# A two-layer transformer kernel: a wide second mixer buffer in dead key and value slots, VectorE score tiles across segment borders, and a new plan

## The chip, the cores and the metric

The kernel runs on one core of one Trainium2 chip. The metric is the time of one launch in device microseconds; the median of several runs counts. The core has five engines that run side by side: TensorE (PE; its weight loads are PEld in the profile), VectorE (DVE), ScalarE (ACT), GpSimd (POOL) and SyncE (SP), which here only issues DMAs.

## The reference

The input x has 2048 rows of 448 values in bfloat16. Two equal layers are run one after the other, each an attention block (16 heads of 28 values) and a mixer block with an MLP:

```python
x = A_x
x = x + _A_ref(_layernorm(x), A_wqkv, A_wo)
x = x + _B_ref(_layernorm(x), B_w1, B_w2, B_w3, B_w4)
x = x + _A_ref(_layernorm(x), A_wqkv, A_wo)
x = x + _B_ref(_layernorm(x), B_w1, B_w2, B_w3, B_w4)

def _A_ref(x, wqkv, wo):            # q, k, v: 16 heads of 28
    scores = einsum("bhqd,bhkd->bhqk", q, k) * (28 ** -0.5)
    o = einsum("bhqk,bhkd->bhqd", softmax(scores), v)
    return o.reshape(B, S, D) @ wo

def _B_ref(x, w1, w2, w3, w4):
    h = gelu(layernorm(x) @ w1)     # then four column groups of h, moved by
    hs = shifted(h) @ w2            # +1, -1, +2, -2 rows, with zeros at the ends
    x1 = x + hs
    return x1 + gelu(layernorm(x1) @ w3) @ w4      # w3: 448 x 1792, w4: 1792 x 448
```

## The kernel before

The 2048 rows are 16 tiles of 128 rows. Heads go in 4 groups of 4. The queries are cut into five chunks (of 4, 4, 4, 2 and 2 tiles), and keys are taken in passes, so that attention can begin before all keys exist; one chunk, one head group and one pass make a **segment**. There are 28 segments in layer one (0 to 27) and 36 in layer two (28 to 63). A segment has one block for each 512 columns of scores and head: a key tile for a chunk of 4 query tiles, two key tiles for a chunk of 2.

*The stream of scores.* `t_scores` walks the segments in order and takes units of 3 and 2 score tiles of 128x512 in turn (banks 0 to 2, 3 and 4 of PSUM). `score_ops` issues their matmuls (L1300). `t_exp` (L1455) lets ScalarE take the exponential of each unit, PSUM to the buffer PT. `t_pv` multiplies with the values (L761; its buffer named PT or PD) into bank 5. `t_norm` copies the sums out (L1534, L1536) and, after the last pass of a chunk, divides, mostly through two DMAs and a product on GpSimd (L1560), in the last chunk of layer two through TensorE.

*Tiles for VectorE.* Beside a unit, `t_scores` may take one or two more score tiles for VectorE: it looks 5 to 6 blocks ahead (DLO, DHI) **in the same segment**, only for chunks of 4 tiles, and only if TensorE's planned fillers of the last 8 us make up a share of at least FTH. It takes one if fewer tiles of the segment were taken than the rate D_RATE times (block + 1) times 4, and if a free bank (b6, b7), an integer buffer (`yd`, 2) and an output buffer (`PD`, 4) are at hand. `d_first` (L1341) brings the scores out of PSUM as fixed-point numbers, and `d_chain` (L1362, L1364, L1366, L1369) works the exponential out as a polynomial on the low half and an exponent from the high half: five VectorE instructions. The chain has the priority DPRIO until its block is near, then 1.0.

*The mixers.* When a chunk is done in all four head groups, `t_outproj` multiplies with wo and adds to x; `t_mixA` (LayerNorm, w1, gelu through a tanh, L1684 to L1704) works on the chunk, `t_mixB` on groups of 3, 4, 4, 2 and 3 tiles, whose rows need their neighbours: the shifted product with w2 (x1b, L1772), LayerNorm (L967), transposing, w3 into `h2T` (evacuated by VectorE, L1837), one long gelu on ScalarE over the whole buffer (L1852; it needs another activation table, loaded before and after), and w4. There is one `h2T` of 14 x 512 columns. In layer two the group of 2 tiles uses instead a buffer `h2V` of 14 x 256 columns in value slots 9 to 15, which are dead from the end of layer one's attention ("kvfree"). The last group runs after the exponentials, with its hidden values in PT. Each `t_mixA`, `t_mixB`, key and query load holds one of the transposed buffers xT0, xT1 and, after "kvfree", xT2 in key slots 9 to 12.

*Keys and values of layer two.* `kT` and `vaug` have 23 slots of one tile. Layer one uses 0 to 15; layer two puts its tiles 0 to 6 into 16 to 22 and 7 to 15 into 0 to 8. So slots 16 to 22 are empty in most of layer one, and 9 to 15 in layer two. `t_kv` loads transposed tiles by a DMA on SP's queue; `k_proj` makes keys (evacuation L1110, squares on GpSimd L1096, their sum on TensorE, the maximum on VectorE L1121), `v_proj` the values.

*The plan.* All of this is written as Python generators, and a planner (`Sched`) orders their instructions in one list for each engine before the launch. It has a duration for each instruction, margins for what other engines deliver late (DOUBT, DOUBT2), a rank for each part (RANK: 'a' and 'b' the mixer halves, 'k' and 'q' the projections, by layer and index; lower goes first), a lead for the queries (Q_LEAD) and a share of TensorE's recent 2.3 us that must be work (TARGET). Where TensorE would be idle below that share, `keep_pe_busy` puts in a **filler** (L1893): four small matmuls into a bank that nobody uses.

## Time and profile before

| | |
|---|---|
| median of 8 runs | 1077.35 us (1076.23 to 1081.22) |
| the profiled execution | 1077.18 us |
| its span | 1075.5 us |
| granted TensorE clock, mean | 0.998 |
| exponentials L1455 | 805 instructions, 920.8 us on ScalarE |
| long gelus L1852 on h2T | 8 instructions, 41.9 us |
| table loads beside them | 8 before a gelu and 8 before an exponential, 1283 ns each |
| fillers L1893 | 3804 matmuls, 166.7 us |
| tiles on VectorE, L1341 | 37 |
| waits of ScalarE's exponentials for scores | 13.2 us in 10 waits, the longest 4.0 |

A row of the profile's groups gives the line, the engine and the operation, the tile written and those read, the shape and the count; then the busy time, the mean duration of one, and the idle time of the engine just before such instructions. Durations of neighbours overlap a little, so a busy time is less than count times mean. A row of stretches gives the busy time of each engine between two times, counted from the start of the span.

### The profile page before, as it was taken

To read this page: it belongs to the slowest core of one execution; us is meant where nothing else is said; L and a number is where in the kernel's file an instruction comes from. 1 tells how busy PE (TensorE), PEld (TensorE's weight loads), DVE (VectorE), ACT (ScalarE), POOL (GpSimd) and SP (SyncE) were. 2 spreads that over 40 slices of the span, in tenths; PEclk is the share of its full clock that TensorE was granted. 3 is DMA by queue.
4 is the path that set the end of the run, shared out by engine and by line. 5 is a ranking of instruction groups with operands and counts; after the bars stand their busy time and mean duration, and the time that the engine had idled before them with its cause. 6 is when DMAs were issued, how large, how long until landed. Compare 5 with 4: busy or idle time off the path is not lost.

```text
span 1075.5 us, 35352 instructions
## 1 busy us (share of the span) xinstructions
PE 1007.6 (94%) x16034; PEld 422.4 (39%) x16037; DVE 619.0 (58%) x1236; ACT 1020.7 (95%) x920; POOL 314.0 (29%) x506
## 2 busy tenths in 40 slices
PE   6899999999999999999999998999999999999998
PEld 2333443443333433343433433353333433444455
DVE  7776579836468336755156553514797484444442
ACT  6898999999999999999999999999999999999952
POOL 2244126201254024452042201102753130432111
PEclk9999999999999999999999999999999999999999
DMA  3547221103111022120221122413411110220000
GB/s 115 138 111 209 81 57 32 23 17 91 32 32 32 13 83 52 44 42 22 63 58 40 45 90 86 132 56 103 90 27 21 42 40 16 59 49 16 12 11 32
DMA packets 95494, 62.26 MB, mean 58 GB/s; under 512 B 68528, under 2 KB 85248, under 8 KB 95344
## 3 DMA queue, kind: packets, MB, share of 16 engines
q1 hardware_dynamic: 91968, 51.92, 18.8%
q0 software_dynamic: 3376, 8.09, 2.7%
q8 instruction: 125, 2.05, 0.8%
q14 instruction: 25, 0.20, 0.1%
HBM read 27.12 MB, written 15.71 MB: 40 GB/s over the span
## 4 chain that ended last, share of the span: by engine, by line
ACT 65%; PE 21%; DVE 11%; DMA 2%; issue 1%; POOL 0%; SPq 0%; DVEq 0%
ACT PT L1455 58%; PE ps L770 11%; PE ps L1300 5%; PE ps L761 4%; ACT h2T L1852 4%; DVE fb L1364 1%; DMA rT<-ub 1%; ACT fb L1703 1%; DVE PD L1369 1%; DVE fb L1362 1%; PE ps L1893 1%; ACT L1455 1%; ACT L1852 1%; DVE yd L1341 1%; DVE qT L1143 1%
## 5 line engine op out<-in xcount | busy, mean ns | idle before, releaser
L1455 ACT ACTIVATE PT<-ps 128x1536 bf16<-128x1536 f32 (+1 forms) x805 | 920.8, 1335 | 14.4 <-PE ps L1300 13.2
L1300 PE MATMUL ps<-qT,kT 32*128 32x512 bf16 (+1 forms) x2560 | 315.0, 340 | 29.4 <-ACT PT L1455 20.2
L761 PE MATMUL ps<-PT,vaug 128*32 128x512 bf16 (+1 forms) x2523 | 250.3, 340 | 0.0
L1300 PEld LDWEIGHTS ps<-qT,kT 32*128 32x128 bf16 x2560 | 80.7, 91 | 300.1 <-ACT PT L1455 272.9
L1893 PE MATMUL ps<-ident 128*32 128x256 bf16 x3804 | 166.7, 274 | 3.0 <-POOL ident L850 1.5
L770 PE MATMUL ps<-xT,w 128*32 128x512 bf16 (+2 forms) x1600 | 126.3, 360 | 2.8 <-DVE h2T L1837 1.4
L1893 PEld LDWEIGHTS ps<-ident 128*32 128x32 bf16 x3804 | 108.2, 96 | 30.3 <-issue 12.3
L770 PE MATMUL ps<-w,h2T 128*32 128x448 bf16 x1512 | 104.5, 359 | 13.8 <-ACT h2T L1852 12.9
L1837 DVE CAST h2T<-ps 128x512 bf16<-128x512 f32 (+2 forms) x112 | 67.9, 606 | 79.5 <-PE ps L770 69.9
L761 PEld LDWEIGHTS ps<-PT,vaug 128*32 128x32 bf16 x2523 | 74.7, 95 | 93.5 <-issue 80.2
L1560 POOL TENSOR_TENSOR otn<-ub,fb 128x512 bf16<-128x512 f32 (+1 forms) x36 | 40.6, 1128 | 183.4 <-DMA fb<-rscr 183.2
L1096 POOL TENSOR_TENSOR sq<-kT 128x512 bf16<-128x512 bf16 (+2 forms) x32 | 29.9, 937 | 120.4 <-DVE kT L1110 120.2
L770 PEld LDWEIGHTS ps<-xT,w 128*32 128x32 bf16 (+1 forms) x1600 | 43.7, 95 | 42.9 <-issue 17.9
L770 PEld LDWEIGHTS ps<-w,h2T 128*32 128x32 bf16 x1512 | 40.6, 97 | 50.8 <-issue 17.0
L1701 POOL TENSOR_TENSOR fb<-hT 112x512 f32<-112x512 bf16 (+1 forms) x36 | 37.4, 1042 | 78.2 <-DVE hT L1684 74.5
L1341 DVE TENSOR_SCALAR yd<-ps 128x512 int32<-128x512 f32 x37 | 25.1, 683 | 39.3 <-PE ps L1300 38.9
L1787 POOL TENSOR_TENSOR x_res<-x_res,x1b 128x448 f32<-128x448 f32 x32 | 38.9, 1224 | 20.9 <-DVE xn L967 19.3
L1534 DVE COPY ub<-ps 128x512 f32<-128x512 f32 (+1 forms) x40 | 23.3, 583 | 36.1 <-PE ps L761 35.8
L953 POOL TENSOR_SCALAR vpe<-mv 128x1 f32<-128x1 f32 (+2 forms) x21 | 5.5, 262 | 128.1 <-DVE mv L948 128.1
L1852 ACT ACTIVATE h2T<-h2T 128x7168 bf16<-128x7168 bf16 (+2 forms) x8 | 41.9, 5244 | 0.1
L1536 DVE SCALAR_TENSOR_TENSOR ub<-ub,fct,ps 128x512 f32<-128x512 f32 x24 | 17.9, 747 | 41.0 <-PE ps L761 40.7
L770 PE MATMUL ps<-kT,w 128*32 128x512 bf16 (+2 forms) x576 | 40.4, 360 | 0.8 <-DMA kT<-xn 0.7
(168 smaller groups left out, 1206.5 us busy)
## 6 DMA issues: line engine op xcount, KB each, us to landing
uscr<-ub SPq DMA_DIRECT2D x24, 256.0 KB
ub<-uscr SPq DMA_DIRECT2D x24, 256.0 KB
fb<-rscr SPq DMA_DIRECT2D x24, 256.0 KB
xnd<-xn SPq DMA_DIRECT2D x28, 128.0 KB, 2.2
x_res<-in_A_x_dram POOLq DMA_DIRECT2D x16, 224.0 KB, 4.2
xd<-x_res SPq DMA_DIRECT2D x16, 224.0 KB, 2.7
x_res<-xd SPq DMA_DIRECT2D x16, 224.0 KB, 3.6
out_dram<-obf SPq DMA_DIRECT2D x16, 112.0 KB
```

The lines of the kernel that those rows point to most:

```text
L761: return lambda e: e.matmul(out=out, lhsT=lhsT, rhs=rhs, start=start, stop=stop, **kw)
L770: r.append(e.matmul(out=out[c:c + w, :], lhsT=lhsT[:, c:c + w], rhs=rhs, start=start, stop=stop, tile_position=(0, c)))
L1096: return op("pool", 0.15 + NW * 0.0018, lambda e: e.tensor_tensor(out=sq[:, si, 0:NW], in0=src, in1=src, op=ALU.mult), reads=rk, writes=[( ...
L1300: yield op("pe", max(0.055, 0.22 / nc_ * NW / 512.0), lambda e, i=i, kc=kc, j=j, g=g, a=a, NW=NW, bank=bank: e.matmul(out=ps[:, bank, i * ...
L1341: yield op("dve", c_ps(512), lambda e: e.tensor_scalar(out=y, in0=ps[:, bi(bank), :], scalar1=SCALE * L2E * FS, scalar2=-126.0 * FS, op0=A ...
L1455: yield op("act", 0.06 + n * w * 0.000833, lambda e, bk=bk, s0=s0, n=n, w=w: e.activation(out=PT[:, s0:s0 + n, 0:w], in_=ps[:, bk[0]:bk[0] ...
L1560: yield op("pool", 0.2 + NW * 0.0021, lambda e: e.tensor_tensor(out=otn[:, g, 0:NW], in0=u, in1=rb[:, 0:NW], op=ALU.mult), reads=[uk, fk], ...
L1701: yield op("pool", 0.2 + NW * 0.00165, lambda e: e.tensor_tensor(out=f, in0=z, in1=z, op=ALU.mult), reads=hk, writes=[fk])
L1787: yield op("pool", 1.2, lambda e: e.tensor_tensor(out=X, in0=X, in1=X1, op=ALU.add), reads=[xk, ("x1b", s)], writes=[xk], deps=[nop_])
L1837: ev = op("dve", c_ps(NW), lambda e, fch=fch, b=b: e.tensor_copy(out=hb[:, fch, 0:NW], in_=ps[:, bi(b), 0:NW]), reads=[("ps", bi(b))], wri ...
L1852: yield op("act", c_act(nl * NW), lambda e: e.activation(out=hb[:, 0:nl, 0:NW], in_=hb[:, 0:nl, 0:NW], func=ACT.Gelu_apprx_tanh), reads=al ...
L1893: return [e.matmul(out=ps[32 * c:32 * c + 32, bi(b), 0:256].rearrange("p (a n) -> p a n", n=128), lhsT=ident[:, 32 * c:32 * c + 32], rhs=i ...
```

## The change

1. **A wide second buffer.** `h2V` goes. `t_mixB` of either size takes `h2T` or, once it exists, `h2W`: 14 x 512 columns, the first 7 in value slots 9 to 15 and the other 7 in key slots 9 to 15 of the four groups. Its long gelu is two instructions, one for each half.
2. **Dead slots lent to VectorE.** `t_extra` lends 7 value slots as two integer buffers, one float buffer and one output buffer: slots 16 to 22 from the start to segment 20, and 9 to 15 from "kvfree" to segment 58. At the end of the first loan GpSimd writes the padding again (two memsets), and only then do layer two's first two key groups begin ("xdone", 0). At the end of the second, xT2 is taken as well and no longer given out; only then does `h2W` exist.
3. **Tiles across borders.** With DSEG = 1 the look 5 to 6 blocks ahead goes on into the next segment, if its keys and queries are there. The code of a chain on GpSimd comes in too, but all of its rates (PRATE) are 0. One more memset (`dcol`) belongs to it.
4. **A new plan.** RANK, Q_LEAD, D_RATE, DPRIO, FTH, TARGET, AGED and DOUBT2 have other values. `PENORM` is written differently with the same values for these chunks.

The core of the diff (the two RANK lists in full; the chain on GpSimd and what only renames is left out):

```diff
-DPRIO = 5
+DPRIO = 1.5
 DST = [('dve', 0.6), ('dve', 0.6), ('dve', 0.34), ('dve', 0.6)]
 PLAG = 2
 PTS = 1.5
-DSEG = 0
+DSEG = 1
 PFLY = 2
 PBACK = 1.0
 PRATE = {(0, 0): 0, (0, 1): 0, (0, 2): 0, (0, 3): 0, (1, 0): 0, (1, 1): 0, (1, 2): 0}
-XSHUT = (10, 50)
+XSHUT = (20, 58)
 DLO = 5
 DHI = 7
 DPK = 2
-RANK = {k: round(1.1 + 0.05 * i, 3) for i, k in enumerate([('b', 0, 0), ('a', 0, 0), ('k', 0, 1), ('b', 0, 1), ('k', 0, 2), ('k', 1, 0), ('q', 0, 2), ('q', 0, 1), ('k', 1, 2), ('a', 0, 1), ('k', 1, 1), ('q', 0, 3), ('q', 1, 0), ('b', 0, 3), ('k', 0, 3), ('q', 1, 1), ('a', 0, 2), ('b', 0, 4), ('b', 0, 2), ('a', 0, 3), ('a', 0, 4), ('k', 1, 4), ('b', 1, 0), ('a', 1, 0), ('a', 1, 3), ('k', 1, 3), ('a', 1, 4), ('a', 1, 2), ('a', 1, 1), ('b', 1, 4), ('q', 1, 2), ('b', 1, 3), ('q', 1, 3), ('b', 1, 2), ('b', 1, 1)])}
-Q_LEAD = {(0, 1): 6, (0, 2): 9, (0, 3): 3, (1, 0): 7, (1, 1): 9, (1, 2): 4, (1, 3): 5}
-D_RATE = {(0, 0): 0.08, (0, 1): 0.05, (0, 2): 0.05, (0, 3): 0.06, (1, 0): 0.16, (1, 1): 0.1, (1, 2): 0.16}
+RANK = {k: round(1.1 + 0.05 * i, 3) for i, k in enumerate([('b', 0, 1), ('b', 0, 0), ('a', 0, 0), ('k', 1, 0), ('q', 0, 1), ('k', 0, 1), ('q', 0, 3), ('k', 1, 2), ('k', 0, 2), ('q', 0, 2), ('a', 0, 1), ('k', 1, 1), ('q', 1, 0), ('b', 0, 3), ('k', 0, 3), ('q', 1, 1), ('a', 0, 2), ('a', 0, 3), ('k', 1, 4), ('b', 0, 4), ('b', 0, 2), ('a', 0, 4), ('a', 1, 0), ('a', 1, 3), ('b', 1, 4), ('b', 1, 0), ('a', 1, 2), ('k', 1, 3), ('a', 1, 1), ('q', 1, 2), ('b', 1, 2), ('a', 1, 4), ('b', 1, 3), ('q', 1, 3), ('b', 1, 1)])}
+Q_LEAD = {(0, 1): 7, (0, 2): 7, (0, 3): 3, (1, 0): 7, (1, 1): 7, (1, 2): 4, (1, 3): 5}
+D_RATE = {(0, 0): 0.08, (0, 1): 0.045, (0, 2): 0.05, (0, 3): 0.045, (1, 0): 0.015, (1, 1): 0.1, (1, 2): 0.03}
 PE_NORM = {(0, 0): False, (0, 1): False, (0, 2): False, (0, 3): False, (0, 4): False, (1, 0): False, (1, 1): False, (1, 2): False, (1, 3): False, (1, 4): True, (1, 5): True}
 TANHW = {(0, 0): 0, (0, 3): 0, (0, 7): 0, (0, 11): 0, (0, 13): 0, (1, 0): 0, (1, 3): 0, (1, 7): 0, (1, 11): 0}
-Sched.AGED = 0.1
-Sched.TARGET = 0.64
+Sched.AGED = 0
+Sched.TARGET = 0.6
...
-FTH = 0.03
+FTH = 0.15
...
-Sched.DOUBT2 = {"dma": 1.5, "pool": 0.5, "dve": 0, "act": 0.7, "pe": 0.0}
+Sched.DOUBT2 = {"dma": 1.5, "pool": 0.2, "dve": 0.5, "act": 0.5, "pe": 0.0}
...
-            return XT + (["xT2"] if ("third",) in SC.events else [])
+            return XT + (["xT2"] if ("third",) in SC.events and ("xshut", 1) not in SC.events else [])
...
+            if L == 1 and c < 2:
+                yield ("wait", ("xdone", 0))
...
+        def xtra(kind):
+            for ph, base in ((0, 16), (1, 9)):
+                if ("xopen", ph) in SC.events and ("xshut", ph) not in SC.events:
+                    return {"y": ["yv%d" % base, "yv%d" % (base + 2)], "f": ["fv%d" % (base + 4)], "pd": ["pv%d" % (base + 6)]}[kind]
+            return []
+
+        def t_extra(ph, base):
+            yield ("wait", ("vinit",) if ph == 0 else ("kvfree",))
+            yield ("sig", ("xopen", ph))
+            yield ("wait", ("segstart", XSHUT[ph]))
+            yield ("sig", ("xshut", ph))
+            for r in ("yv%d" % base, "yv%d" % (base + 2), "fv%d" % (base + 4), "pv%d" % (base + 6)):
+                yield ("acq", [r])
+            if ph == 1:
+                yield ("acq", ["xT2"])
+                yield op("pool", 0.2, lambda e: e.memset(vaug[:, 9:16, 0:1], 0.0), reads=[("xT", 2)], writes=[("vaug", s) for s in range(9, 16)] + [("kT", g, s) for g in range(4) for s in range(9, 16)])
+            if ph == 0:
+                pads = vaug[:, base:base + 7, :].rearrange("p t (h r) -> p (t h) r", r=32)
+                wk = [("vaug", base + k) for k in range(7)]
+                yield op("pool", 1.0, lambda e: e.memset(pads[:, :, 28:32], 0.0), writes=wk)
+                yield op("pool", 0.5, lambda e: e.memset(pads[:, :, 28:29], 1.0), writes=wk)
+            yield ("sig", ("xdone", ph))
+
+        def vbuf(r):
+            s = int(r[2:])
+            return vaug[:, s:s + 2, :].rearrange("p a b -> p (a b)"), [("vaug", s), ("vaug", s + 1)]
...
+                past = at[0] > si or (at[0] == si and at[1] >= kb - DURG) or (at[0] == si - 1 and at[1] >= len(seg_kb[si - 1]) + kb - DURG)
+                return 1.0 if past else DPRIO
...
-                rate = DRATE(L, ch, g)
-                if rate and CHUNKS[L][ch][1] == 4 and SC.idle_share(8.0) >= FTH:
-                    for kb in range(kb0 + DLO, min(kb0 + DHI, nkb)):
...
+                for kind in ("pool", "dve"):
+                    if kind == "pool" and SC.cur["pool"] > SC.clock + PBACK:
+                        continue
+                    if SC.idle_share(8.0) < FTH:
+                        continue
+                    lag = PLAG if kind == "pool" else 0
+                    for ahead in range(DLO + lag, DHI + lag):
+                        si, kb = si0, kb0 + ahead
+                        while si < len(segs) and kb >= len(seg_kb[si]):
+                            kb -= len(seg_kb[si])
+                            si += 1
+                        if si > si0 + DSEG or si >= len(segs):
+                            break
+                        L, ch, g = segs[si][0:3]
+                        rate = (DRATE(L, ch, g) if kind == "dve" else PRATE.get((L, ch), 0)) if CHUNKS[L][ch][1] == 4 else 0
...
-                        if taken.get(si, 0) >= rate * (kb + 1) * 4:
+                        if taken.get((si, kind, 0), 0) >= rate * (kb + 1) * 4:
...
+                        if si > si0 and (("q", L, CHUNKS[L][ch][0] // 4, g) not in SC.events or (not segs[si][5] and ("qp", si) not in SC.events)):
+                            break
+                        got = yield ("try", [MISC[0:2], xtra("y") + YS, xtra("pd") + PDS])
...
-            side = not direct and L == 1 and n == 2
-            hname = "h2V" if side else "h2T"
+            wide = False
             if direct:
                 hb, hkey = PT, [[("pt", f)] for f in range(14)]
-            elif side:
-                yield ("wait", ("kvfree",))
-                yield ("acq", [hname], [("xT", xt)])
-                hb = vaug[:, 9:16, :].rearrange("p a b -> p (a b)").rearrange("p (f c) -> p f c", c=256)
-                hkey = [[("vaug", 9 + f // 2)] for f in range(14)]
             else:
-                yield ("acq", [hname], [("xT", xt)])
-                hb, hkey = h2T, [[("h2T", f), ("xst",)] for f in range(14)]
+                hname = yield ("acq", ["h2T", "h2W"] if ("xdone", 1) in SC.events else ["h2T"], [("xT", xt)])
+                wide = hname == "h2W"
+                if wide:
+                    hkey = [[("vaug", 9 + f)] if f < 7 else [("kT", g, 2 + f) for g in range(4)] for f in range(14)]
+                else:
+                    hb, hkey = h2T, [[("h2T", f), ("xst",)] for f in range(14)]
...
+                    parts = [(vaug[:, 9:9 + min(nl, 7), 0:NW], range(min(nl, 7)))]
+                    if nl > 7:
+                        parts.append((kT[:, 0:n, 128 * 9:128 * (2 + nl)], range(7, nl)))
+                else:
+                    parts = [(hb[:, 0:nl, 0:NW], range(nl))]
+                for (v, fr_) in parts:
+                    allk = [k for f in fr_ for k in hkey[f]]
+                    yield op("act", c_act(len(fr_) * NW), lambda e, v=v: e.activation(out=v, in_=v, func=ACT.Gelu_apprx_tanh),
+                             reads=allk, writes=allk, tab="gelu")
...
+        SC.spawn(t_extra(0, 16), 3)
+        SC.spawn(t_extra(1, 9), 3)
...
```

## The prediction

> **What bounds the kernel now.** I read the page first, then the busy time of each engine by stretch, then the filler matmuls (L1893) and VectorE's score tiles (L1341) in the same stretches, and last what ScalarE waits for.
>
> ```profile
> span 1075.5 us, 35352 instructions
> ...
> PE 1007.6 (94%) x16034; PEld 422.4 (39%) x16037; DVE 619.0 (58%) x1236; ACT 1020.7 (95%) x920; POOL 314.0 (29%) x506
> ```
>
> The profiled execution took 1077.18 us, 1.7 us more than its span, and stands 0.2 us under the median of the 8 runs (1077.35). ScalarE and TensorE both look full. The stretches tell them apart (columns: stretch and length; busy us of PE, PEld, DVE, ACT, POOL; clock; DMA share; GB/s):
>
> ```profile
> 20.00:88.00 68.00, 62.75 (x878) 21.99 (x878) 51.30 (x119) 58.40 (x56) 22.67 (x29) 1.00 0.49 130
> 88.00:385.00 297.00, 279.88 (x4442) 114.95 (x4445) 187.29 (x329) 296.00 (x258) 88.20 (x126) 1.00 0.20 50
> 385.00:628.00 243.00, 232.58 (x3650) 95.37 (x3647) 136.12 (x289) 241.85 (x217) 77.91 (x134) 0.99 0.21 53
> 628.00:768.00 140.00, 131.58 (x2081) 54.65 (x2078) 56.47 (x123) 138.19 (x120) 30.23 (x51) 1.00 0.34 96
> 768.00:892.00 124.00, 116.77 (x1774) 44.68 (x1775) 93.82 (x163) 122.11 (x109) 43.57 (x59) 1.00 0.15 33
> 892.00:1027.00 135.00, 126.31 (x2237) 58.25 (x2233) 61.80 (x126) 134.88 (x116) 35.32 (x67) 1.00 0.13 30
> 1027.00:1076.00 49.00, 45.52 (x858) 27.27 (x850) 17.50 (x37) 16.13 (x34) 9.74 (x21) 1.00 0.07 23
> ```
>
> From 88 to 1027 us ScalarE idles 1.0 + 1.2 + 1.8 + 1.9 + 0.1 = 6.0 us of 939: there the exponentials set the time. After 1027 they are over; ScalarE is at 16 of 49 us, and TensorE works through what is left of the last mixers. How much of TensorE is real work, the fillers show (PE and PEld busy time of L1893):
>
> ```profile
> 88.00:385.00 297.00, 76.13 (x1708) 48.90 (x1708) 1.00 0.20 50
> 385.00:628.00 243.00, 18.55 (x484) 13.73 (x484) 0.99 0.21 53
> 628.00:768.00 140.00, 35.83 (x752) 22.06 (x752) 1.00 0.34 96
> 768.00:892.00 124.00, 17.50 (x428) 11.53 (x428) 1.00 0.15 33
> 892.00:1027.00 135.00, 12.55 (x312) 8.85 (x312) 1.00 0.13 30
> 1027.00:1076.00 49.00, 0.00 (x0) 0.00 (x0) 1.00 0.07 23
> ```
>
> So TensorE has 26% to spare in 88:385 and in 628:768, 8% in 385:628, 14% in 768:892, 9% in 892:1027, and nothing in the tail. The tail is bounded by TensorE's leftover work.
>
> VectorE's tiles by stretch (its busy time in L1341, one instruction a tile):
>
> ```profile
> 88.00:385.00 297.00, 16.26 (x24) 1.00 0.20 50
> 385.00:628.00 243.00, 0.69 (x1) 0.99 0.21 53
> 628.00:768.00 140.00, 0.00 (x0) 1.00 0.34 96
> 768.00:892.00 124.00, 8.14 (x12) 1.00 0.15 33
> ```
>
> 37 in all. None in 628:768, though a quarter of TensorE is filler there: those passes have segments of 4 and 5 blocks, and a tile had to lie at least 5 blocks ahead in its own segment.
>
> **What one tile is worth.** Between 240.94 and 311.32 us, 62 exponentials ran without a gap in 70.38 us, alternately 3 and 2 tiles: 155 tiles, 0.454 us each. A tile given to VectorE takes 0.454 us from ScalarE and costs VectorE 0.69 + 0.68 + 0.68 + 0.42 + 0.69 = 3.16 us (medians of L1341, L1362, L1364, L1366, L1369), beside ScalarE's work; VectorE is busy for 63%, 56%, 40% and 76% of the four stretches.
>
> **Score tiles across borders.** I count what the rates allow (a segment stops when its tiles reach rate x (block+1) x 4) and take a share. 88:385: 4 segments of 8 blocks at 0.08 (3 each), 4 of 16 at 0.045 (3), 4 of 16 at 0.05 (4): 40 allowed, 44 before, of which 24 were taken. With the heads of segments open and twice the input buffers I take 30. 385:628: 4 + 12 allowed; fillers at 8% of the time lie under the new threshold of 15% of 8 us, so 2. 628:768: 4 + 4 at 0.015 and 8 + 8 at 0.1, 24 allowed; fillers at 26% pass, but none lie in 628:645, so 10. 768:892: the rate falls from 0.16 to 0.03, 8 allowed, fillers near the threshold: 6 for 12. Together 48 for 37: 11 x 0.454 = **-5.0 us**. Bounds: all 88 allowed would be 51 x 0.454 = -23 us; if the threshold of 0.15 (it was 0.03) shuts out half of my 48, 24 tiles are +6 us. I take the middle, because the stretches with room have fillers well over the threshold on average.
>
> **Priority of VectorE's chains (5 to 1.5).** They now go ahead of mixer work ranked later. The 11 new tiles bring 11 x 3.16 = 35 us to an engine with 456 us free: nothing, by that cover. Without it each chain instruction ahead of an evacuation that TensorE waits for is 0.7 us, and a fifth of 48 chains so placed some 7 us; this end is kept for the range.
>
> The trace has these chains meet something: L1364 takes 684 ns in the median and 1762 at worst, L1362 659 to 1626. The Trainium skill ("SBUF — State Buffer", "Reading the diagram" of the two sides) says that a VectorE instruction with two SBUF inputs and a GpSimd one that reads SBUF exclude each other for a whole instruction. Three of the five operations are such, which speaks against more tiles. By that rule 33 more instructions, meeting a GpSimd one of about 1.1 us in 29% of cases, add some 11 us to VectorE (an estimate); by the medians, 0. Either way it is VectorE's time, and ScalarE's sum stays.
>
> **Fewer fillers (target 0.64 to 0.60).** Filler is TensorE time that real work can use; ScalarE's idle time bounds the gain at 6.0 us in the body, and I take 0. The risk is the clock: in 520:525 the granted clock fell to 0.66 after TensorE had been busy for 2.8 of 5 us, and ScalarE lost 0.8 us there. Eight long gelus give such pauses, so at most 6 us; I take +0.5.
>
> **Layer two's first keys and values.** They now wait for segment 20, whose first 256-wide scores start at 389.3, and for two memsets on GpSimd, estimated in the planner at 1.5 us together. In the trace layer two's first keys (L1110, 128x384) are written between 272.9 and 284.6. The work moved behind 389: keys 64 and squares 16 matmuls at 8.0 us/192 = 0.042, values 48 at 4.5 us/84 = 0.054: 5.9 us of TensorE (rates of the tail, 1055:1065 and 1045:1055). With it go one transposing load on SP's queue, four squares on GpSimd (about 0.9 us each by L1096's mean of 937 ns) and on VectorE four evacuations and four maxima (0.62 and 0.56) and three value copies (about 0.6): 6.5 us. All of it goes into 385:628, whose 18.6 us of fillers and idle VectorE (44%) and GpSimd (68%) cover it, so nothing; without the cover, 5.9 us. Behind GpSimd's memsets queue the squares and the LayerNorm scalars, for which VectorE waits; 1.5 us once. ScalarE's alternative to a late evacuation is not in the sum.
>
> **Second wide buffer, third transposed buffer.** The new buffer opens only after segment 58 starts. In the trace the last matmuls from h2T for the group of tiles 3 to 6 run until 943.8, and the next group's first at 960.6, after its LayerNorm (last L967 at 955.3). So h2T was not what that group waited for; and tiles 11 and 12 had a half-width buffer of their own. I expect 0. In return xT2 ends at segment 58, and two transposed buffers serve the mixers that had three: 0, bounded by -3 us (part of the 12.6 us of fillers in 892:1027 used) and +8 us (below). Ranks and leads are a new order of the same work; 0, inside the same bounds.
>
> Sum: -5.0 + 0.5 = -4.5, so 1077.2 - 4.5 = **1072.7 us**.
>
> **Rivals.**
> (a) *The tail exposes its chain: slower.* The new ranks put the last chunk's output projection and first mixer half behind the second half of tiles 7 to 10. In the trace the chain from 1027 (projection 1033, LayerNorm, w1, gelu, w2 at 1044, transposes, w3 to 1062.8, w4) is covered by 168 matmuls of h2T and 112 of vaug, about 15 us, while it waits. If these go first, the chain's waits stand bare at the end: VectorE idles 4.6 us before L1772 alone, and there are three such steps, some 8 us. It decides once over half of those 15 us run ahead of the projection. With the tiles' gain half gone: 1077.2 - 2.5 + 8 = 1083. For it: no filler in the tail, so order is all. Against: the projection waits on segment 63 anyway.
> (b) *Keys late: slower.* Layer two's last keys, head group 0, are done at 685.7 and their scores start near 694: 8 us of room. If the moved 5.9 us and the priorities make the chain over 8 us late, ScalarE waits; at 14 us late it is +6: with the tiles of 88:385 (-2.7), 1080.5.
> (c) *It doesn't do what it says.* The threshold and the lower rates leave about 37 tiles: 1077.2 + 0.5, no change.
> (d) *More than I count:* 65 tiles, -12.7, and 3 us of the tail: 1062.
>
> **Chances.** Forecast 0.42; (a) 0.20; (b) 0.16; (c) 0.14; (d) 0.08. A measurement of this kernel tells some 0.2% (2.2 us) from no change, so faster means under 1075.2, slower over 1079.5. The forecast's own range, 1068 to 1077, gives 0.37 to faster and 0.05 to same; (d) is faster; (a) and (b) are slower but for 0.03; (c) is 0.08 same, 0.04 slower, 0.02 faster. Faster 0.47, same 0.16, slower 0.37. The range reaches from 1064 to 1086, which takes in (a) and leaves out the ends of the unknown costs.
>
> **What would show it.** Right: 45 to 52 L1341 instructions, about 10 of them between 628 and 768, ScalarE's exponentials some 5 us shorter, its last one before 1024, and a tail still near 49 us. Wrong: L1341 at 37 or fewer; a gap on ScalarE over 2 us between 385 and 700; a tail over 54 us with fillers in it; a granted clock under 0.95 in more stretches than 520:525.

## The result and the profile after

The kernel after takes **1088.36 us** in the median (1084.32 to 1090.83, 11 runs), the kernel before in the same comparison 1077.12 us; the ratio is 1.0097, with an interval of 1.0083 to 1.011. So the change costs about 1%, where 1072.7 us was forecast, a gain of 0.4%. The profiled execution of after took 1088.61 us; its span is 1086.9 us, 11.4 us more than that of before.

The page of the kernel after opens with these lines:

```profile
span 1086.9 us, 34336 instructions
...
PE 1000.9 (92%) x15498; PEld 407.8 (38%) x15501; DVE 636.2 (59%) x1264; ACT 1020.1 (94%) x919; POOL 313.2 (29%) x510
```

ScalarE's busy time is almost the same as before (1020.1 for 1020.7 us). What the span has more is waiting. The stretches of after (same columns as before; the exponentials now end at 1043):

```profile
88.00:385.00 297.00, 269.25 (x4058) 105.19 (x4050) 188.81 (x334) 285.22 (x253) 85.62 (x121) 0.98 0.20 49
385.00:628.00 243.00, 228.82 (x3567) 92.12 (x3560) 137.95 (x287) 241.85 (x212) 79.84 (x137) 0.99 0.19 49
628.00:768.00 140.00, 130.34 (x2029) 52.79 (x2024) 84.64 (x173) 135.72 (x117) 24.94 (x37) 0.99 0.33 95
768.00:892.00 124.00, 115.52 (x1697) 42.66 (x1685) 79.08 (x139) 120.25 (x108) 50.32 (x78) 0.99 0.22 44
```

In 88:385 ScalarE now idles for 11.8 us (1.0 before), in 628:768 for 4.3 (1.8), in 768:892 for 3.8 (1.9); in 385:628 for 1.2, as before. The loss is in layer one's first half and around the start of layer two's wide passes.

The waits say for what. The first line is from the waits of before, the second from those of after:

```profile
ACT PT L1455 <- PE ps L1300: 13.2, 10, 4.0
```

```profile
ACT PT L1534 <- PE ps L1304: 27.0, 24, 5.2
```

(The exponential of before is L1455, its scores L1300; after the change they are L1534 and L1304.) Exponentials wait for scores, that is, for TensorE. Counted from 90 us on, so without what both kernels lose at the start, the idle time that ends with a score matmul is 3.8 us before and 19.9 us after. I use this sum for all kernels below and call it **the body's waits**.

From first to last exponential ScalarE idles 15.7 us more and is busy 0.5 us less; the tail (what comes after the last exponential) is 43.9 us long for 47.5, so 3.7 us shorter. 15.7 - 0.5 - 3.7 = 11.5 of the 11.4 us; the rest is the first exponential, 0.1 us earlier.

VectorE's tiles (L1386 after) are there, 43 for 37; the rows add up to 44, since one tile at 767.9 lies across a border and counts in two:

```profile
88.00:385.00 297.00, 19.02 (x28) 0.98 0.20 49
385.00:628.00 243.00, 0.69 (x1) 0.99 0.19 49
628.00:768.00 140.00, 5.51 (x9) 0.99 0.33 95
768.00:892.00 124.00, 4.04 (x6) 0.99 0.22 44
```

**The longest new wait** is at 118 us. This is the timeline of after (start, duration, engine, line, operation; in brackets the idle time of the engine before it and what ended it):

```profile
105.82 0.71 SPq L1627 DMA_DIRECT2D rT<-ub  x1
...
115.46 0.34 DVE L1628 RECIPROCAL rT<-rT 64x32 f32<-64x32 f32 x1 [5.80 <-DMA rT<-ub]
115.73 0.64 DVE L1145 TENSOR_SCALAR qT<-ps,bc 128x512 bf16<-128x512 f32 x1
...
116.42 1.05 PE L1989 MATMUL ps<-ident 128*32 128x256 bf16 x16 [4.86 <-DVE qT L1145]
...
118.06 1.45 ACT L1534 ACTIVATE PT<-ps 128x1536 bf16<-128x1536 f32 x1 [5.22 <-PE ps L1304]
```

Read it backwards. ScalarE stands 5.22 us for scores. TensorE stood 4.86 us ahead of a filler, which waits for the query evacuation L1145 on VectorE. That evacuation had nothing to wait for; it stood in VectorE's list behind the reciprocal L1628, and the reciprocal waited for a DMA of 8 KB with the row sums, issued at 105.82 and not there until 115.46: 9.6 us. At five other places of after at which VectorE waits for the same DMA, it takes 1.8 us (183.21 to 184.99 and 215.62 to 217.38, for instance). What lay beside it, the 5-us windows show (columns as in the stretches; the last three are granted clock, DMA share, GB/s):

```profile
105.00:110.00 5.00, 4.66 (x54) 1.34 (x46) 3.38 (x5) 5.00 (x6) 1.91 (x2) 1.00 1.01 341
110.00:115.00 5.00, 1.49 (x24) 0.44 (x21) 0.00 (x0) 2.85 (x3) 0.00 (x0) 0.92 0.82 269
115.00:120.00 5.00, 3.58 (x38) 1.25 (x42) 1.60 (x3) 1.68 (x2) 1.04 (x1) 0.50 0.13 24
```

The loads of w3 and w4 (three DMAs of 3.2 MB together; the expectations below say 2.9 MB, which leaves out the smallest; issued by GpSimd between 102.3 and 104.8) fill the DMA engines for about 10 us. VectorE does nothing from 110 to 115; TensorE is busy for 1.49 of 5 us, and in the next 5 us its granted clock is 0.50.

In the kernel before the same DMA met the same loads:

```profile
104.58 0.71 SPq L1548 DMA_DIRECT2D rT<-ub  x1
...
111.64 0.34 DVE L1549 RECIPROCAL rT<-rT 64x32 f32<-64x32 f32 x1 [3.39 <-DMA rT<-ub]
111.91 0.62 DVE L1172 TENSOR_TENSOR qT<-qT,ps 128x512 bf16<-128x512 bf16 x1
...
112.58 0.84 PE L1893 MATMUL ps<-ident 128*32 128x256 bf16 x24 [0.35 <-DVE qT L1172]
```

There it took 7.1 us and VectorE stood 3.39 us, but TensorE had other work until then and stood only 0.35 us for the instruction behind it; ScalarE lost nothing. So the danger lay open in the profile of before, and the new order moved a query evacuation into it.

### The profile page after: what moved, and what is told of

The parts are those of the page before. It is cut to its first block, busy times and chain, and to the rows that moved or that the text cites. A ratio compares the mean times of both kernels' runs of the same rounds, so it can differ in the third digit from the quotient of the medians.

```text
span 1086.9 us, 34336 instructions
## 1 busy us (share of the span) xinstructions
PE 1000.9 (92%) x15498; PEld 407.8 (38%) x15501; DVE 636.2 (59%) x1264; ACT 1020.1 (94%) x919; POOL 313.2 (29%) x510
## 4 chain that ended last, share of the span: by engine, by line
ACT 63%; PE 23%; DVE 7%; DMA 3%; POOL 1%; issue 1%; SPq 1%; DVEq 0%; POOLq 0%
ACT PT L1534 56%; PE ps L771 11%; PE ps L1304 6%; PE ps L762 5%; ACT h2T L1948 3%; DMA rT<-ub 2%; ACT fb L1782 1%; ACT L1948 1%; ACT L1534 1%; PE ps L1989 1%; DVE ub L1615 1%; DVE vaug L1386 0%; DVE st L949 0%; DMA PT<-in_A_wqkv_dram 0%; DMA xT<-xn 0%
## 5 line engine op out<-in xcount | busy, mean ns | idle before, releaser
L1534 ACT ACTIVATE PT<-ps 128x1536 bf16<-128x1536 f32 (+1 forms) x802 | 920.1, 1323 | 30.6 <-PE ps L1304 27.0
L1304 PE MATMUL ps<-qT,kT 32*128 32x512 bf16 (+1 forms) x2560 | 314.2, 342 | 38.4 <-ACT PT L1534 30.5
L1304 PEld LDWEIGHTS ps<-qT,kT 32*128 32x128 bf16 x2560 | 80.3, 91 | 317.1 <-ACT PT L1534 283.2
L1989 PE MATMUL ps<-ident 128*32 128x256 bf16 x3268 | 152.6, 277 | 8.6 <-DVE qT L1145 4.9
L771 PE MATMUL ps<-xT,w 128*32 128x512 bf16 (+2 forms) x1664 | 131.4, 370 | 3.8 <-DVE hT L1763 1.7
L1989 PEld LDWEIGHTS ps<-ident 128*32 128x32 bf16 x3268 | 93.0, 97 | 38.7 <-issue 13.1
L1639 POOL TENSOR_TENSOR otn<-ub,fb 128x512 bf16<-128x512 f32 (+1 forms) x36 | 41.6, 1156 | 225.9 <-DMA fb<-rscr 220.1
L771 PE MATMUL ps<-w,h2T 128*32 128x448 bf16 x1400 | 95.8, 358 | 10.2 <-ACT h2T L1948 10.1
L1926 DVE CAST h2T<-ps 128x384 bf16<-128x384 f32 (+2 forms) x98 | 58.2, 594 | 74.7 <-PE ps L771 69.2
L771 PE MATMUL ps<-xT,wk_pad 128*32 128x512 bf16 (+2 forms) x576 | 45.1, 365 | 1.1 <-DVE kT L1112 0.6
L1098 POOL TENSOR_TENSOR sq<-qT 128x512 bf16<-128x512 bf16 x28 | 30.0, 1076 | 45.2 <-DVE qT L1145 39.9
L771 PE MATMUL ps<-wv,xT 128*32 128x448 bf16 x512 | 40.6, 366 | 2.0 <-DVE kT L1112 0.5
L771 PE MATMUL ps<-wo_pad,otn 128*32 128x448 bf16 x512 | 40.3, 357 | 1.1 <-DVE x_res L1693 0.9
L771 PE MATMUL ps<-xT,wq_pad 128*32 128x512 bf16 x448 | 38.0, 391 | 2.6 <-DMA xT<-xnd 1.8
```

What stands on the lines that cost most here:

```text
L771: r.append(e.matmul(out=out[c:c + w, :], lhsT=lhsT[:, c:c + w], rhs=rhs, start=start, stop=stop, tile_position=(0, c)))
L1098: return op("pool", 0.15 + NW * 0.0018, lambda e: e.tensor_tensor(out=sq[:, si, 0:NW], in0=src, in1=src, op=ALU.mult), reads=rk, writes=[( ...
L1304: yield op("pe", max(0.055, 0.22 / nc_ * NW / 512.0), lambda e, i=i, kc=kc, j=j, g=g, a=a, NW=NW, bank=bank: e.matmul(out=ps[:, bank, i * ...
L1534: yield op("act", 0.06 + n * w * 0.000833, lambda e, bk=bk, s0=s0, n=n, w=w: e.activation(out=PT[:, s0:s0 + n, 0:w], in_=ps[:, bk[0]:bk[0] ...
L1639: yield op("pool", 0.2 + NW * 0.0021, lambda e: e.tensor_tensor(out=otn[:, g, 0:NW], in0=u, in1=rb[:, 0:NW], op=ALU.mult), reads=[uk, fk], ...
L1926: ev = op("dve", c_ps(NW), lambda e, hr=hr, vw=vw, b=b: e.tensor_copy(out=hr, in_=vw(ps[:, bi(b), 0:NW])), reads=[("ps", bi(b))], writes=h ...
```

## The experiments

Two theories were tested, each with what it expects of the runs. **D** (the DMA): VectorE's list stands at a reciprocal whose row sums are late, an evacuation behind it holds TensorE, and ScalarE waits. **F** (the fillers): with TARGET 0.60 there are 3268 filler matmuls for 3804, TensorE pauses more often and longer, its clock falls, and scores are late. Some kernels edit the finished plan: an instruction is moved in its engine's list behind all that the plan starts before a given time, with all that depends on it; nothing else changes. Others change settings and are planned anew, which can move everything. (In the expectations, theory K stands for the tiles, ranks and late keys, theory O for the mere fact of a new order.) Where a ratio is given, it is to the kernel before in the same comparison; that of after is 1.0097 (1.0083 to 1.011).

**1. All reciprocals later, in both kernels**

```diff
+    for o in [all reciprocals L1628 (before: L1549)]:
+        order = sink(order, o, o.t0 + 5.0)
```

> The changed kernel with its 36 reciprocals of row sums (L1628) and the two DMAs that hang on each moved back in VectorE's and SyncE's lists, behind whatever else the planner starts in the next 5 us; TensorE's and ScalarE's lists stay the same. Theory D (VectorE stands at a reciprocal that waits for its DMA, query evacuations queue behind it, TensorE and then ScalarE wait): the stalls at 118, 748 and 788 us go (6.0 + 1.7 + 1.9 us), so 1079 to 1082 instead of 1088. Theory F (fewer fillers let the clock fall, and slow scores cost the time): within 2 us of 1088. Theory K (tiles, ranks and late keys): within 2 us of 1088.

> The same move of the reciprocals in the kernel before. Theory D: only its one such stall, 1.7 us at 739, goes: 1075 to 1077. Theory F: no change.

After: 1139.47 us, ratio 1.0571 (1.0538 to 1.0603). Before: 1141.04 us, 1.0591 (1.0567 to 1.0615). Set against their own unedited kernels the first loses 51 us, the second 64. The cure was worse than the illness: GpSimd's list holds the product L1639 (L1560) that uses the reciprocal, it stayed where it was, and squares and LayerNorm scalars stood behind it. GpSimd's waits for the DMA ahead of the product (fb) grew from 220.1 to 321.3 us in after and from 183.2 to 283.0 in before. Nothing follows for or against D, except that the division's chain may not be made later as a whole.

**2. Only the reciprocals of head groups 0 to 2 later**, up to 6 us

```diff
+        if n % 4 != 3:
+            order = sink(order, o, o.t0 + 6.0)
```

> The move of a_recip_late, by up to 6 us, for the reciprocals of the first three head groups of a chunk alone (27 of 36); the fourth, on which the output projection hangs, stays. TensorE's and ScalarE's lists stay the same. Theory D: the stall at 118 (6.0 us) and what of 748 and 788 belongs to these groups go: 1079 to 1083. Rival (VectorE's wait at the reciprocal costs nothing that ScalarE does not lose anyway): 1087 to 1090.

> The same for the kernel before, which has stalls of 3.4 and 1.1 us at such reciprocals with ScalarE fed all the same. Theory D: 1075 to 1077. Rival: the same, or slower if the moved chains are late for the output projection.

1129.76 us, 1.0495 (1.0479 to 1.0511), and 1129.51 us, 1.049 (1.0474 to 1.0505). Too blunt for the same reason: GpSimd's waits for fb grew to 304.6 and 260.8 us. What was needed was to touch one place only.

**3. The number of fillers**: after with every sixth filler doubled (+136), before without every seventh (-135)

```diff
+        if fill and DROP and k % DROP == 0:
+            continue
         order.append(o)
+        if fill and TWICE and k % TWICE == 0:
+            order.append(o)
```

> The changed kernel with every sixth filler put in twice (136 more, about as many as the kernel before has); all else in the same order. Theory F: the clock stays up between stalls and 4 to 8 us come back: 1080 to 1084. Theory D: fillers are not what is missing; within 2 us of 1088, and clock dips remain behind the same stalls.

> The kernel before with every seventh filler left out (135 fewer, about as many as the changed kernel has); all else in the same order. Theory F: the clock falls in several places and it loses 4 to 8 us: 1081 to 1085. Theory D: within 2 us of 1077.

After with more: 1085.35 us, 1.0095 (1.0062 to 1.0128); the body's waits fall from 19.9 to 16.2 us, the wait at 118 stays at 5.06, the one at 206 shrinks from 2.15 to 0.50. The ratio is that of after within its interval: not decided. Before with fewer: 1077.55 us, 1.0013 (0.9996 to 1.003), where F had 4 to 8 us of loss. A smaller number of fillers alone costs that kernel nothing that shows.

**4. Settings and code exchanged**: the code of before with the eight new settings, and the code of after with the eight old ones (RANK, Q_LEAD, D_RATE, DPRIO, FTH, AGED, TARGET, DOUBT2)

```diff
-DPRIO = 5
+DPRIO = 1.5
...
-Sched.TARGET = 0.64
+Sched.TARGET = 0.6
```

> The code of the kernel before (no borders crossed, no lent slots, half-width second buffer) with the new RANK, Q_LEAD, D_RATE, DPRIO, FTH, TARGET, AGED and DOUBT2. If the new numbers cause the loss (the order around chunk 1's query projections, later first keys of layer two): 1083 to 1092. If the features cause it (tiles across borders, lent slots, wide buffer, keys that wait for segment 20): 1074 to 1080.

> The changed code, borders crossed and slots lent, with the old numbers of the same eight settings. If the new numbers cause the loss: 1070 to 1080. If the features cause it: 1084 or more.

New settings on the old code: 1098.71 us, 1.021 (1.0191 to 1.023). Old settings on the new code: 1099.53 us, 1.0208 (1.0189 to 1.0227). Either half alone costs twice what the whole does. Longest waits of the two:

```profile
ACT PT L1455 <- PE ps L1300: 32.2, 17, 12.5
```

```profile
ACT PT L1534 <- PE ps L1304: 47.4, 31, 17.3
```

The 12.5 us (at 711.8) and the 17.3 us (at 707.1) are layer two's last keys, late: what rival (b) of the prediction described. The tail is longer as well, 54.7 and 53.5 us for 47.5 before and 43.9 after. The second has 68 tiles on VectorE, and its exponentials take 907.6 us of ScalarE for 920.1 in after; body's waits of 39.1 us and the tail take more than that back. And the wait at 118 is in the first (5.03 us) and not in the second: it comes with the settings, that is, with the order, not with the buffers.

**5. The place at 118 alone, from two sides.** In one kernel the loads of w3 and w4 go some 50 us later in GpSimd's list; in the other only the first reciprocal goes behind the query evacuation that followed it.

```diff
+    for key in ("w4", "w3"):
+        for o in [loads of key]:
+            order = sink(order, o, o.t0 + 55.0)
```

```diff
+    order = sink(order, first_reciprocal, first_reciprocal.t0 + 1.6)
```

> The changed kernel with the loads of w3 and w4 (2.9 MB, first needed after 200 us) about 50 us later in GpSimd's list; every other list stays the same. Theory D with its cause (the first row-sum DMA, 8 KB, takes 9.6 us because these loads run beside it): that DMA lands within 3 us, the stall of 5.2 us at 118 goes and what follows it: 1081 to 1084. Rival (the DMA is late for another reason): 1087 to 1090, the stall stays.

> The changed kernel with only the first of the 36 reciprocals moved, behind the one query evacuation that follows it in VectorE's list; all else as it was. Theory D: the evacuation no longer stands behind the late DMA, TensorE's filler and scores go on, and the stall at 118 shrinks from 5.2 to under 2 us: 1083 to 1086. Rival: the stall stays, because the next evacuation waits as well: 1087 to 1090.

1083.01 us, 1.0068 (1.0042 to 1.0095), and 1083.65 us, 1.0061 (1.003 to 1.0093). With the loads out of the way the DMA takes 3.8 us at most (105.64 to the reciprocal at 109.40, for which VectorE no longer waits), and the wait at 118 is gone. In the second kernel the DMA is as late as ever, but the evacuation passes it:

```profile
109.94 0.75 DVE L1145 TENSOR_SCALAR qT<-ps,bc 128x512 bf16<-128x512 f32 x1 [0.18 <-PE ps L771]
...
115.55 0.35 DVE L1628 RECIPROCAL rT<-rT 64x32 f32<-64x32 f32 x1 [4.86 <-DMA rT<-ub]
```

VectorE still stands 4.86 us, and ScalarE has no wait near 118. So D holds here: neither the DMA nor VectorE's pause costs anything by itself, only what is queued behind. The body's waits are 14.6 us with the loads later and 17.6 with the reciprocal moved. Both kernels get back 3 to 4 us by their ratios; their intervals overlap that of after a little, so the size is uncertain, and what shows D is the wait that is gone in both.

**6. TARGET exchanged**

```diff
-Sched.TARGET = 0.6
+Sched.TARGET = 0.64
```

> The changed kernel with TARGET 0.64, planned anew. If the fillers' number is the cause: 1080 to 1084. Theory O: anywhere from 1080 to 1100, with stalls in other places than at 118.

> The kernel before with TARGET 0.60 alone, planned anew. If fewer fillers as such cost time: 1080 to 1084. If any new order that was not chosen costs time (theory O): the lists shift throughout and it takes 1080 to 1100. If neither: 1076 to 1079.

After with 0.64: 1083.18 us, 1.0069 (1.0041 to 1.0097), an interval that overlaps that of after. The plan has 91 fillers more (364 matmuls); the other instructions are the same, and in the same order on every engine but for two places on VectorE (156 to 161 and 330 to 354 us) and TensorE's instructions beside them. The wait at 118 stays (5.10); those at 206, 359, 502 and 924 fall below 0.4 us each; in layer two 1.49, 1.71 and 1.55 us remain at 744, 773 and 777, and one of 0.64 at 878 is new. The body's waits are 15.4 us, 4.5 less. What a filler does shows best ahead of 206, where the order is the same. In after VectorE's late work leaves TensorE idle for 1.03 us until 201.9, and then:

```profile
202.89 2.82 PE L771 MATMUL ps<-w,hT 112*32 112x448 bf16 x24
...
200.00:205.00 5.00, 3.59 (x49) 1.60 (x48) 4.39 (x8) 4.15 (x5) 0.51 (x1) 0.79 0.02 3
```

With 0.64 the pause is filled, and the same 24 matmuls run at a granted clock of 1.00:

```profile
202.22 1.51 PE L771 MATMUL ps<-w,hT 112*32 112x448 bf16 x24
...
200.00:205.00 5.00, 5.00 (x92) 2.39 (x84) 4.73 (x9) 4.85 (x6) 0.16 (x1) 1.00 0.01 3
```

The scores stand behind them, and ScalarE's wait is 2.15 us in the first and 0.20 in the second.

Before with 0.60: 1077.19 us, 1.0007 (0.999 to 1.0024). So F holds for the kernel after by its waits, though fewer fillers cost the kernel before nothing: they matter where other stalls have already made pauses.

**7. Both cures together, and a control**: after with the loads later and TARGET 0.64; before with the loads later.

> The kernel after, planned with TARGET 0.64 instead of 0.60, and with the 2.9 MB of w3 and w4 loads some 50 us later in GpSimd's list. The two edits alone gave 1083.18 (-5.2 us) and 1083.01 (-5.4). If they take away two different things (the DMA that VectorE stands for at 115; the clock that falls after short pauses of TensorE), the sum holds: 1088.4 - 10.6 = 1078, 1077 to 1080, with no gap of over 2 us on ScalarE between 100 and 300. If both are one thing (fewer pauses of TensorE, whatever ends them), 1082 to 1083.

> The kernel before, with the w3 and w4 loads some 50 us later in GpSimd's list; a control. There the row-sum DMA at 104.58 took 7.0 us too and VectorE stood for 3.39 us, but nothing that the scores wait for stood behind it. If that is why it cost nothing: 1077, within 1.5 us, with that DMA near 2 to 3 us. If the loads slow something else in general, faster by 4 to 5 us: 1072 to 1073.

After with both: **1076.47 us, 1.0 (0.9986 to 1.0015)**. The whole loss is gone. The body's waits are 8.5 us; 19.9 - 5.3 (loads) - 4.5 (fillers) = 10.1 would be left if the two simply added up, so they do at least that. Against the loads alone (1.0068) the step to 0.64 is clear of the noise here. Of the eleven 5-us windows before the last in which after's clock lay under 0.97 one is left (760:765, 0.69). ScalarE's waits for scores, the start included:

```profile
ACT PT L1534 <- PE ps L1304: 15.3, 16, 4.3
```

The control went as neither expectation had it: 1082.75 us, 1.0065 (1.0048 to 1.0082), slower. At the old place the first reciprocal starts at 107.45 without a wait; the timeline further on shows the new one:

```profile
150.38 1.13 POOL L817 DMA_DIRECT2D w<-in_B_w_dram  x1
...
151.65 0.49 SPq L1551 DMA_DIRECT2D rscr<-rT  x1
...
157.96 0.53 SPq L1556 DMA_DIRECT2D fb<-rscr  x1
...
163.95 1.26 POOL L1560 TENSOR_TENSOR otn<-ub,fb 128x512 bf16<-128x512 f32 x1 [12.44 <-DMA fb<-rscr]
...
165.26 0.94 PE L770 MATMUL ps<-wo_pad,otn 128*32 128x448 bf16 x8 [5.23 <-POOL otn L1560]
...
166.78 2.48 ACT L1455 ACTIVATE PT<-ps 128x1536 bf16<-128x1536 f32 x2 [5.71 <-PE ps L1300]
```

Moved by 50 us, the loads met another step of the same division, in the last head group of a chunk: the 8 KB to rscr took 6.3 us (issued 151.65; the next DMA, which needs it, went out at 157.96), the one after it up to 6 us more, GpSimd's product came late, TensorE's output projection with it, and ScalarE lost 5.71 us. The same price at another place, this time in the kernel before: it is the meeting of a bulk load with a chain that the scores stand behind, whatever the kernel. In after with the loads later the same meeting is milder: only one of the three loads (1.4 MB) stands ahead of that product, the DMA to rscr takes 5.6 us (151.69 to 157.33), TensorE's projection waits 1.84 us, and ScalarE 1.17 and 1.03 us at 164 and 167. That much of the gain at 118 the new place takes back.

**8. A second place for D, and the worth of the tiles.** In one kernel, with the loads later, the reciprocals for which VectorE stood at 746, 775 and 785 (2.01, 4.16, 2.75 us) go behind the evacuations that followed them; in the other only DSEG goes back.

```diff
+    for n in (23, 26, 27):
+        order = sink(order, rec[n], rec[n].t0 + 1.6)
```

```diff
-DSEG = 1
+DSEG = 0
```

> The kernel after, with the loads later and with three reciprocals of layer two, those for which VectorE stood 2.01, 4.16 and 2.75 us at 746, 775 and 785, put some 1.6 us later in VectorE's list, behind the evacuations that followed them. ScalarE's gaps at 748, 774 and 788 came to 1.09 + 0.61 + 1.28 + 1.51 + 0.37 = 4.9 us. If VectorE's list is the cause there as at 118: 1083.0 - 4 = 1079, 1077.5 to 1080.5, and those gaps under 0.5 us each. If a late reciprocal holds up GpSimd's list as the 5 us did: 1084 or more.

> The kernel after, planned with DSEG 0: VectorE's tiles only within a segment, everything else as it is. The plan has some 10 tiles fewer on VectorE. If a tile is worth what it takes from ScalarE, 10 x 0.454 = +4.5: 1093, 1091 to 1096. If the tiles across borders cost by their VectorE work in front of evacuations as much as they bring, 1086 to 1090. If they are what made the kernel slower, 1077 to 1083.

The three reciprocals: 1083.94 us, 1.0071 (1.0052 to 1.0091), no better than the loads alone, and the body's waits are 17.5 us for 14.6. VectorE no longer stands at these three for more than 0.4 us. ScalarE's wait of 1.28 us at 744 is gone, as D has it. But 1.26 and 1.13 us remain at 773 and 775, and TensorE shows for what:

```profile
772.17 0.62 PE L771 MATMUL ps<-xT,wq_pad 128*32 128x512 bf16 x8 [1.77 <-DMA xT<-xnd]
...
773.15 1.02 ACT L1534 ACTIVATE PT<-ps 128x1024 bf16<-128x1024 f32 x1 [1.26 <-PE ps L1304]
```

The next queries' transposing load is late, and its matmuls stand ahead of the scores. So D is *not* the cause of these waits. The trace of after has the same row (1.79 us for that load, at 773.19); I had laid the wait to the reciprocal that stood nearby. A new wait of 1.39 us at 757, ahead of which VectorE stood 3.00 us for the next reciprocal, took back what was won at 744; others of 1.05, 0.56 and 0.91 us came at 359, 362 and 482.

Without tiles across borders: 1098.73 us, 1.0213 (1.0182 to 1.0243), with 33 tiles (27, 1, 0 and 5 in the four stretches). The body's waits are 23.9 us, 4.0 more, with a new one of 6.19 at 579; the one at 118 stays (4.90). The span of 1098.3 us is 11.4 longer than that of after: ScalarE idles 3.7 us more, is busy 2.2 more (ten tiles at 0.454 would be 4.5) and has its first exponential 0.4 later, and the tail is 5.1 us longer (49.0). So nothing here says that the tiles across borders made the kernel slower; what they are worth by themselves this run can't say, since without them the planner builds another order.

**9. The priority of VectorE's chains, and more fillers still**

```diff
-DPRIO = 1.5
+DPRIO = 5
```

```diff
-Sched.TARGET = 0.6
+Sched.TARGET = 0.68
```

> The kernel after with DPRIO 5 as before, planned anew: VectorE's chains give way to the mixers again. By the prediction's step (chains have VectorE's idle time as cover, their priority is worth nothing) 1088, 1086 to 1090, with the stall at 118 as it was, since no chain stood there. If the chains ahead of evacuations cost the 7 us that the prediction kept as an end, 1081. A new order may bring new stalls of its own; then over 1090, and the gaps on ScalarE say where.

> The kernel after with the loads later and TARGET 0.68 instead of 0.64, planned anew. With 0.64 it took 1076.5 with one low stretch of the clock left (760 to 765, 0.69). If fillers only guard the clock, there is little left to win: 1075 to 1077. If more fillers stand in the way of real work, or the new order brings stalls, 1079 or more.

DPRIO 5: 1095.57 us, 1.0183 (1.0155 to 1.0211), with 44 tiles; the wait at 118 is there (5.02 us), and there are ones of 2.74 us at 503 and 3.47 us at 704 (keys again). In sum the body's waits are 20.6 us, hardly more than in after; what makes this order longer is the tail, 49.3 us for 43.9. So nothing here says that the new priority made the kernel slower. TARGET 0.68 with the loads later: 1091.12 us, 1.0132 (1.0105 to 1.0159), 28 waits of 21.7 us in the body and a tail of 53.8 us. Here the planner built another order (41 tiles, other waits from 134 to 1021), so this tells of the order and not of fillers. A version clearly faster than both kernels was not found.

## Why the prediction was wrong

**The step that failed** is the one sentence "Ranks and leads are a new order of the same work; 0, inside the same bounds". An order has a price of its own: which instruction stands behind one that waits for a DMA. The profile of before had the row (VectorE 3.39 us at 111.64 for a DMA of 7.1 us beside 3.2 MB of loads), and I counted the engines' busy time instead of asking what might come to stand behind it. It cost 5.2 us of waiting at 118; two edits of that place alone took the wait away and gave back 3 to 4 us of time. Two terms of the sum were mis-sized besides, the fillers and the tiles.

**Fewer fillers**: taken at +0.5, bounded by 6. Giving them back brings 3.0 us by the ratios with the stall in place (1.0097 to 1.0069), 7.3 with the loads moved (1.0068 to 1.0); each of these ratios is uncertain by 2 to 3 us, and only the second gain is clear of that. I had looked for pauses beside the long gelus. Most were beside the new stalls: under 0.97 stood the windows 65:70, 110:125, 200:210, 500:505, 745:755, 785:790 and 920:925, and only 520:525 before. So the term belongs near its upper bound or past it (4.5 us of waits); its mechanism was right, its size and its place wrong.

**Tiles**: 43 instead of 48, by stretches 28, 1, 9 and 5 for my 30, 2, 10 and 6. The counting worked. But ScalarE's work fell by 0.5 us only, not by 6 x 0.454 = 2.7, nor by the 5.0 of the sum. The price of 0.454 was that of an unbroken row, where 62 exponentials of 1.335 us in the mean follow each other every 1.135 us; each break loses the 0.20 of overlap, and there are 13 breaks more, 2.6 us (an estimate, which no run tests). A price taken from an unbroken row holds only while the row stays unbroken.

**Priority of the chains**: nothing, with an end of 7 us. No sign that it cost anything (experiment 9).

**First keys of layer two**: nothing, and in 385:628, where their work was moved to, ScalarE is busy for 241.85 us in both kernels. Right.

**Wide buffer, xT2**: nothing. The eight long gelus cost the same, one now in two halves of 3.2 us at 1024 and 1027, and nothing waits for the buffer. The tail got 3.7 us shorter. I had bounded that at -3 to +8 and counted 0; whether the buffer or the new order shortened it, no run separates.

**Rivals.** (a) is wrong, and in its sign: the tail is shorter. It is a danger of other orders, though: in six of the kernels planned anew the tail is 49.0 to 54.7 us. (b) is half right: the last keys leave a wait of 2.44 us at 702.88 in after, since their last evacuation is done at 700.5, so the 8 us of room are used up; that is far from the 14 us of lateness that (b) needed, and not the main loss. In the exchanged kernels of experiment 4 it was 12.5 and 17.3 us. Of the signs that I had named for a wrong prediction, the clock under 0.95 came true, and the gap of over 2 us lies just past the 700 that I had set.

**The sum as it came**: 1077.2 + 16.1 (body's waits, 19.9 - 3.8) - 0.5 - 3.7 = 1089.1, for 1088.6 measured in that execution. The sum of the prediction had -5.0 for the tiles, +0.5 for the clock, nothing for other waits and 0 for the tail. Of the 16.1, 5.3 go with the loads moved and 4.5 with the fillers, separately; both together take 11.4, and with the shorter tail that makes a kernel as fast as before. Of the 8.5 us that are then left, 2.44 are the last keys and 3.4 lie between 736 and 764, where a late query load stands (TensorE idles 1.95 us ahead of its matmuls at 760.72); no run took those away.

What stays open: how much of the loss by the fillers elsewhere is matmuls at a lower clock, as at 206, and how much the pauses themselves; and why the two cures together give back 10.4 us of time by the ratios and singly 3.1 and 3.0. The intervals of the single ones are wide enough for either.

## What to carry to other kernels

In an engine that works through its list in order, look for every instruction that waits for a DMA, and ask of a new order what it puts *behind* it; a pause of 3 us that costs nothing today is a stall of 5 us tomorrow. Bulk loads that no one needs yet are best placed by what runs beside them, not by when the buffer is free: here 50 us later won some 3 us in one kernel and lost 7 in the other. Spare fillers, worthless in a kernel whose TensorE hardly pauses, pay in one that has short stalls; that a stall and a missing filler make each other worse is likely here and not shown.

## What the runs showed of the hardware

An 8 KB DMA took 1.8 us with little beside it and 6.3 to 9.6 us beside loads that held the DMA share at 0.82 to 1.03 for most of that time. Bulk loads aren't the only cause: in layer two of after the same DMA took 4.7 us (issued 741.61) and 5.3 us (779.93) at a share of 0.18 and 0.17, for reasons that no run settles. The Trainium skill ("DMA: Bandwidth & Descriptors", "Anatomy of one DMA — SWDGE (gpsimd) path") gives a DMA a fixed part of about 2.0 us that scales with nothing, plus its bytes at 436 GB/s, so 2.0 us for 8 KB, an estimate. The undisturbed 1.8 us come near it, though these DMAs come from SP's queue; beside the loads the estimate fails, and the measurement decides.

TensorE's clock fell after pauses: in after it was 0.50 in the window behind one in which TensorE had been busy for 1.49 of 5 us, with a pause of 4.86 us. Short pauses were enough, too: 0.66 in 785:790, whose longest pause was 1.75 us, and 0.67 in 500:505, behind pauses of 0.46 and 0.52 us in a window in which TensorE was busy for 4.02 of 5. The Trainium skill ("TensorE: Matmul & The Clock Gate", "HAM oscillation — how this bites in real kernels") tells of waits that cross the window in which activity is counted and let each next piece of work start at half clock; the row of 115:120, 0.50 behind the pause of 4.86 us, agrees.
